# Statistics of the fourth row tile on ScalarE, those of the sixth and eighth on VectorE, and other ordering rules

## The chip, the cores and the metric

The kernel runs on one core of a Trainium2 chip. The engines are TensorE (PE, matmuls; PEld is its weight load), VectorE (DVE), ScalarE (ACT), GpSimd (POOL) and SyncE (SP, which issues DMAs). The metric is the device time of one execution in microseconds. Before the change it is 691.98 us, the median of three runs (691.73 to 692.18).

## The reference

One residual block on x of 2048 rows and 640 columns (bf16). The rows are normalised, and the result goes both through attention with 32 query heads of 20 columns and one shared key and value head, and through a two-layer network with silu:

```python
x = A_x
xn = _layernorm(x, axis=-1)
return x + _A_ref(xn, A_wq, A_wk, A_wv, A_wo) + _B_ref(xn, B_w1, B_w2)
```

In `_A_ref`, `q = xn @ wq` is split into 32 heads, `k = xn @ wk`, `v = xn @ wv`, `scores = q k^T * 20 ** -0.5`, and softmax over 2048 keys is taken before the product with v and with `wo`. In `_B_ref`, `h = silu(xn @ w1)` with 1728 columns, then `h @ w2`. The layernorm has no weights: `(x - m) / sqrt(v + 1e-5)`.

## The kernel before, in words

**Tiling.** The 2048 rows are 16 row tiles of 128, numbered from 0, and four query chunks of 512. Heads go in eight groups of four, each head in a slot of 32 rows, so that four score matmuls (`s_mm`, L1078) run side by side in TensorE. A unit of work is one key tile with one head: 128 keys by 512 queries, which fills one of the eight PSUM banks.

**The exponentials** are made on two ways. On ScalarE one ACTIVATE (L1166) takes two or three neighbouring banks, so 1024 or 1536 columns. On the other way a batch of four heads is turned by VectorE into integers that are read as bf16 (L1409, one head each), and two shifted copies of it are added, by GpSimd (L1448) or VectorE (L1453); the three together approximate the exponential, so such a batch needs three products with v where a batch of ScalarE needs one. The product with v is L1201 (`pv_mms`).

**Other matmuls.** Projections and the two layers go through `col_mm` (L447); `row_mm` (L454) is another cut of the same products that runs beside score matmuls. In the beginning each row tile is normalised, transposed (L595), copied into `xnT` by ScalarE for tiles 0 and 1 (L604) and by VectorE for the rest (L607); from that come kT (L621, copied by ScalarE at L631, and for tiles 1 to 3 by VectorE at L629), the first queries (L668, copied at L672), v (L645, L653) and the other queries (L447, L693). At the end stand the sums of the last head groups (copy L1302, matmuls L999, L1017) and the output layer (L919, L967, L984). Where TensorE would idle and has streamed little, a filler (L1725) multiplies zeros.

**The layernorm** (`ln_pair`) works on two row tiles at a time. A tile's statistics are made on VectorE (two BN_STATS, L563 and L565, one BN_AGGR, L567), or, for tiles in `ACT_LN`, on ScalarE: two ACTIVATEs with a sum over the row (L552, L554), after which VectorE scales the mean (L557). Then VectorE adds epsilon (L570), GpSimd takes the power -0.5 (L572), for tiles from 4 on VectorE forms a bias (L577), and the tile is normalised: tiles 0 to 3 by VectorE (L588), the others by GpSimd (L585). A pair goes on only when both of its tiles have their statistics. The ring of normalised tiles holds five.

**The order** of all instructions on every engine is made when the kernel is built. A list scheduler steps through modelled time, with a cost for each operation and a priority (`prio`), and picks the next operation of the engine that is earliest. TensorE's choice follows numbers in `BASE` (how long to keep a bank, how far products may lag, when to open a new sum). Every 10 us of modelled time (`PIECE`) the numbers are set anew: `BASE` with the exceptions in `RULES` that the letter of `PLAN` at that place names. Each engine then runs its list in order, with semaphore waits where another engine's result is needed. So a change to `PLAN`, or to the work of the beginning, makes another order for the whole kernel: which units go to ScalarE and which to VectorE, in which widths, and what stands between them on TensorE.

```python
while not finished():
    if sc.t["pe"] >= piece * PIECE:
        ru.__dict__.update(BASE)
        ru.__dict__.update(RULES[rule(piece)])
        piece += 1
```

The functions that the diff touches, with the line numbers of the profile:

Of the kernel before, what the change touches and what calls it, by code (L numbers as in the profile page):

```python
# [69 lines left out]
LOOK = 30.0  # L70
LOOK0 = 100.0
LOOK1 = 200.0
LNP = {1: ((4, 2), (6, 2)), 2: ((8, 2), (10, 2)), 3: ((12, 2), (14, 2))}
DVE_NORM = ()
PS = 1.0
# [23 lines left out]
AHEAD = 1  # L99
QAT = (0, 1)  # L100
TRN = 2
ACT_LN = (5, 7)
TRACT = (0, 1)

BASE = dict(uopen=4, umin=3, uleft=3, uwait=500.0, pace=-1.0, lagl=3, half=6, hold2=0, bnd=4, pj=6000.0, rows=0, rowmin=3, lagmax=6, lagp=0, lagj=6, openlag=5, late=-0.02, lead=0.01, leadmax=0.02, need=640.0, hold=300.0, dwant=600.0, slack=700.0, dnow=400.0, hungry=0.0, patience=0.0, keep=460.0, open=2, zcap=9, stay=0.0, homes=1, want=1, claim=6)
RULES = dict(a={}, b=dict(keep=0.0), c=dict(lagp=3), d=dict(lagp=5), e=dict(lagp=0), f=dict(patience=200.0), g=dict(dwant=0.0),
             h=dict(zcap=4), i=dict(zcap=3), j=dict(homes=0), k=dict(leadmax=-1.0, lead=-1.0), l=dict(lead=0.08, leadmax=0.1),
             m=dict(need=740.0), n=dict(hold=0.0), o=dict(stay=640.0), p=dict(open=1), q=dict(slack=560.0), r=dict(hungry=1000.0), s=dict(claim=9), t=dict(open=3), u=dict(claim=4), v=dict(want=2), w=dict(slack=850.0), x=dict(hold2=4), y=dict(bnd=0), z=dict(pj=-1e9), A=dict(rows=0), B=dict(rows=2, rowmin=2), C=dict(pj=2000.0), D=dict(openlag=3), E=dict(pj=8000.0), F=dict(hold2=3), G=dict(rows=1), H=dict(half=0), I=dict(half=3), J=dict(stay=560.0), K=dict(stay=720.0), P=dict(need=560.0), Q=dict(hold=120.0), L=dict(uopen=3), M=dict(uopen=4), N=dict(uopen=5), O=dict(uopen=0))
PLAN = "acbtJKazNvhaJvxvixrrnrKzDDnQDmoqvknpfLBGvDPmoJdftFQdkttaQBBoknQEaoz"


def rule(n):
    return PLAN[n] if n < len(PLAN) else "a"
PACE = 1.0
# [214 lines left out]
def build(nc, A_x, A_wq, A_wk, A_wv, A_wo, B_x, B_w1, B_w2, out, stack):  # L329
# [185 lines left out]
    def wrow(ap):  # L515
        return ap.rearrange("(c p) d -> p c d", p=P)
# [30 lines left out]
    def ln_pair(n0, k):  # L547
        aggs = []
        an = [n for n in range(n0, n0 + k) if n in ACT_LN]
        for n in an:  # L550
# [40 lines left out]
    def tr_job(n):  # L591
        mms = []
        for c in range(DC):
            def f(pe, b, c=c, n=n):
                return pe.transpose(bk16(b)[:, c * P:(c + 1) * P], xn_ring[n % XNR][:, c * P:(c + 1) * P],  # L595
                                    ident_b[:, :])
            mms.append((f, 65.0, "f", [norm_op[n], idb], [res("xn", n % XNR), res("idb")]))
        job = pe_job(f"tr{n}", mms, 550)

        def src(b):  # L600
            return bk16(b)[:, 0:DC * P].rearrange("p (c t) -> p c t", c=DC)
        dst = xnT[:, :, n * P:(n + 1) * P]
        if n in TRACT:
            op = Op("act", lambda a: a.activation(dst, src(job.bank), AF.Copy), t_act(640), ACT_END, pre=[job.ready],  # L604
                    writes=[res("xnT", n)], prio=-1.0, job=job)
        else:
            op = Op("dve", lambda v: v.tensor_copy(dst, src(job.bank)), 412, DVE_END, pre=[job.ready],  # L607
                    writes=[res("xnT", n)], prio=0.2 if n < 4 else PT, job=job)
        job.consumers = [op]
        xnT_op[n] = op  # L610
        return job
# [3 lines left out]
    def kT_job(t0, t1):  # L615
        mms = []
        parts = [(i, i + 1) for i in range(t0, t1)] if t1 <= 4 else [(t0, t1)]
        for a, b_ in parts:
            for c in range(DC):
                def f(pe, b, c=c, a=a, b_=b_):  # L620
                    return pe.matmul(bk(b, (a - t0) * P, (b_ - t0) * P), wk_sb[:, c, :], xnT[:, c, a * P:b_ * P],  # L621
                                     start=(c == 0), stop=(c == DC - 1))
                mms.append((f, t_mm((b_ - a) * P), "f", [xnT_op[i] for i in range(a, b_)] + wk_cp, [res("wk")]))
        job = pe_job(f"kT{t0}", mms, 1100)
        n = (t1 - t0) * P
        dst = kT_rep[:, t0 * P:t1 * P]
        args = dict(pre=[job.ready], writes=[res("kT", i) for i in range(t0, t1)], job=job)
        if t0 == 1:
            op = Op("dve", lambda v: v.tensor_copy(dst, bk(job.bank, 0, n)), t_dve(n), DVE_END, prio=0.25, **args)  # L629
        else:  # L630
            op = Op("act", lambda a: a.activation(dst, bk(job.bank, 0, n), AF.Copy), t_act(n), ACT_END, prio=-1.5, **args)  # L631
        job.consumers = [op]
        for i in range(t0, t1):
            kT_op[i] = op
        return job
# [27 lines left out]
    def q0_job(t0):  # L663
        mms = []
        for i in range(t0, t0 + 2):
            for c in range(DC):
                def f(pe, b, c=c, i=i):
                    return pe.matmul(bk(b, (i - t0) * P, (i - t0 + 1) * P), wq_pad[:, c, :], xnT[:, c, i * P:(i + 1) * P],  # L668
                                     start=(c == 0), stop=(c == DC - 1))
                mms.append((f, t_mm(P), "f", [xnT_op[i], wqp0], []))  # L670
        job = pe_job(f"q0_0{t0}", mms, 1100)
        op = Op("dve", lambda v: v.tensor_scalar_mul(qT[:, 0, t0 * P:(t0 + 2) * P], bk(job.bank, 0, 2 * P), QSCALE), t_dve(256), DVE_END,  # L672
                pre=[job.ready], writes=[res("qT", 0, 0, t0)], prio=0.2, job=job)
        job.consumers = [op]
        q_op.setdefault(0, []).append(op)
        q_res.setdefault(0, []).append(res("qT", 0, 0, t0))
        return job
# [797 lines left out]
    def pro_fill():  # L1475
        for kc in range(4):
            if kc == 0:
                ln_pair(0, 2)
                ln_pair(2, 2)
            else:  # L1480
                for a, k in LNP[kc]:
                    ln_pair(a, k)
            trs = []
            for n in range(4 * kc, 4 * kc + 4):
                j = tr_job(n)
                tr_ops[n] = j.ops
                trs.append(j)
            if kc == 0:
                ka, kb, qa, qb = kT_job(0, 1), kT_job(1, 4), q0_job(0), q0_job(2)
                ka.fixed, qa.fixed = ABUFS[1]  # L1490
                trs[2].fixed, trs[3].fixed, qb.fixed = ABUFS[0]
                pro.extend(Piece(j) for j in trs[:TRN])
                pro.append(Piece(ka))
                pro.append(Piece(qa, qa.ops[:DC]))
                pro.extend(Piece(j) for j in trs[TRN:])
                pro.append(Piece(qa, qa.ops[DC:]))
                pro.append(Piece(qb, qb.ops[:DC]))
                pro.append(Piece(qb, qb.ops[DC:]))
                pro.append(Piece(kb))
            else:  # L1500
                pro.extend(Piece(j) for j in trs)
                pro.append(Piece(kT_job(4 * kc, 4 * kc + 4)))
            pro.append(Piece(v_job(kc)))
            for k in range(2):
                if kc == QAT[k]:
                    pro.append(Piece(q_job(0, k)))
            if kc == 0:
                d_w["w1"] = dma("w1", lambda e: e.dma_start(w1_sb[:, :, :], wrow(B_w1)), D * F * 2, writes=[res("w1")],
                                prio=1.0)
                nf = (FC - 1) * P  # L1510
                d_w["w2a"] = dma("w2a", lambda e: e.dma_start(
                    w2_sb[:, 0:FC - 1, :], B_w2[0:nf, :].rearrange("(c p) d -> p c d", p=P)), nf * D * 2,
                    writes=[res("w2a")], prio=1.1)
                d_w["w2"] = dma("w2", lambda e: e.dma_start(w2_sb[0:FLAST, FC - 1, :], B_w2[nf:F, :]), FLAST * D * 2,
                                writes=[res("w2")], prio=1.2, pre=[d_w["w2a"]])
                d_w["w2b"] = dma("w2", lambda e: e.dma_start(w2_sb[FLAST:P, FC - 1, :], B_w2[nf:F, :]), FLAST * D * 2,
                                 writes=[res("w2b")], prio=1.2, pre=[d_w["w2"]])
                d_w["wo"] = dma("wo", lambda e: e.dma_start(wo_sb[:, :, :], wrow(A_wo)), D * D * 2, writes=[res("wo")],
                                prio=1.3)
                for k in range(2 * HG):  # L1520
                    a, r = (H - 2 * HG + k) * DH, k % HG * SLOT
                    d_wo_end.append(dma("wo_end", lambda e, k=k, a=a, r=r: e.dma_start(wo_end[r:r + DH, k // HG, :], A_wo[a:a + DH, :]),
                                        DH * D * 2, pre=[wo_zero], writes=[res("wo_end", k)], prio=1.4))
        for o in [d_w[k] for k in WLATE] + d_wo_end:
            o.pre += q_op[1]
        for i in range(QTP):
            xres_op[(0, i)] = x_ld[i]
# [436 lines left out]
    def step_other(e):  # L1964
        t = sc.t[e]
        best = None
        for op in sc.pools[e]:
            es = sc.est(op)
            if es is None:
                continue  # L1970
            key = (0, op.prio, es) if es <= t + ((LOOK0 if not att["n"] else LOOK if ln_done[0] else LOOK1) if op.prio < LOOKP else 30.0) else (1, es, op.prio)
            if best is None or key < best[0]:
# [201 lines left out]
```

## Time and profile before

| | |
|---|---|
| median of three runs | 691.98 us (691.73 to 692.18) |
| the profiled execution | 691.7 us, its span 689.9 us |
| busy share of the span | PE 98%, ACT 97%, DVE 86%, POOL 85% |
| exponentials on ScalarE | 590 of 1024 columns, 64 of 1536 |
| granted TensorE clock | 1.00 |

The span goes from the first instruction to the last; the profiled execution's own time has 1.8 us around it. A row of a timeline is start, duration (both us), engine, source line, operation, output and input with their shapes, the number of equal instructions merged, and in brackets the idle time before with what ended it. A row of a group ends with the busy time in us, the mean of one in ns, and the idle time before these instructions. A row of waits is total us, how often, and the longest. A row of stretches gives the length, then the busy us of PE, PEld, DVE, ACT and POOL with the number of instructions, the clock, the DMA share and GB/s. Neighbouring instructions of one engine can overlap by the tail of the first, so sums are taken from start to start.

### The profile page before, as it was taken

Reading aid. Unit: us, or ns where it says so; the run is one execution under the profiler, and the core shown is the slowest. Engines: PE = TensorE matmul, PEld = TensorE weight load, DVE = VectorE, ACT = ScalarE, POOL = GpSimd, SP = SyncE. Lnnn points to the kernel's source line nnn. Section 1 sums busy time; section 2 is a strip of 40 time slices with the busy share of each in tenths; the row PEclk is TensorE's granted clock in tenths of the full one; section 3 lists DMA queues with packets and bytes.
Section 4 is the critical chain, followed back from the end, with each engine's and each line's share of the span. In section 5 each row is a group of like instructions: output and inputs, shape, how many; then the busy total and the mean of one; then the engine's idle time right before and its main releaser. Section 6 shows DMA issues by size and latency. Waiting matters only on the chain.

```text
span 689.9 us, 22614 instructions
## 1 busy us (share of the span) xinstructions
PE 676.4 (98%) x9870; PEld 234.4 (34%) x9873; DVE 594.7 (86%) x1017; ACT 665.9 (97%) x726; POOL 583.9 (85%) x351
## 2 busy tenths in 40 slices
PE   8999999999999999999999999999999999999998
PEld 5432222322233333323233333322232333333345
DVE  7899989988998867898988888798988889989973
ACT  6999999999999999999999999999999999999990
POOL 6668899898988889898899899989889998888860
PEclk9999999999999999999999999999999999999999
DMA  7753221122221232321212223222222202223201
GB/s 217 178 180 42 20 20 15 33 35 30 18 28 12 31 40 30 69 34 17 33 14 30 29 31 40 23 65 29 29 19 22 22 18 32 31 23 68 23 7 41
DMA packets 34241, 28.97 MB, mean 42 GB/s; under 512 B 15486, under 2 KB 29662, under 8 KB 34142
## 3 DMA queue, kind: packets, MB, share of 16 engines
q1 hardware_dynamic: 33854, 27.20, 25.7%
q8 instruction: 77, 1.26, 0.8%
q10 hardware_dynamic: 288, 0.33, 0.1%
q14 instruction: 22, 0.18, 0.1%
HBM read 11.09 MB, written 2.62 MB: 20 GB/s over the span
## 4 chain that ended last, share of the span: by engine, by line
PE 76%; ACT 16%; DVE 4%; POOL 1%; SPq 1%; DMA 1%; issue 1%; DVEq 0%; ACTq 0%
PE psall L1201 26%; PE psall L1078 25%; PE psall L447 23%; ACT sbt L1166 14%; DVE sbt L1409 1%; ACT sbt L773 1%; POOL sbt L1448 1%; SPq L706 1%; DMA sbt<-sbt 0%; PE psall L621 0%; DVE sbt L563 0%; PE psall L734 0%; DVE sbt L607 0%; PE psall L1725 0%; DVE sbt L565 0%
## 5 line engine op out<-in xcount | busy, mean ns | idle before, releaser
L1166 ACT ACTIVATE sbt<-psall 128x1024 bf16<-128x1024 f32 (+1 forms) x654 | 643.0, 1156 | 2.3 <-PE psall L1078 2.1
L1448 POOL TENSOR_SCALAR sbt<-sbt 128x2048 int16<-128x2048 int16 x275 | 521.7, 1897 | 70.4 <-DVE sbt L1453 22.4
L1409 DVE TENSOR_SCALAR sbt<-psall 128x512 int16<-128x512 f32 x676 | 441.8, 685 | 64.4 <-PE psall L1078 60.1
L1078 PE MATMUL psall<-sbt 32*128 32x512 bf16 x2048 | 269.2, 384 | 4.3 <-ACT sbt L1166 1.6
L1201 PE MATMUL psall<-sbt 128*32 128x512 bf16 x3400 | 264.8, 384 | 0.6 <-POOL sbt L1448 0.4
L447 PE MATMUL psall<-sbt 128*32 128x320 bf16 (+3 forms) x3792 | 227.6, 332 | 2.5 <-DVE sbt L1409 0.8
L1078 PEld LDWEIGHTS psall<-sbt 32*128 32x128 bf16 x2048 | 71.4, 91 | 238.8 <-ACT sbt L1166 172.7
L447 PEld LDWEIGHTS psall<-sbt 128*32 128x32 bf16 (+1 forms) x3792 | 82.4, 95 | 82.7 <-issue 44.7
L1201 PEld LDWEIGHTS psall<-sbt 128*32 128x32 bf16 x3400 | 70.1, 94 | 114.5 <-issue 71.0
L1453 DVE TENSOR_SCALAR sbt<-sbt 128x2048 int16<-128x2048 int16 x63 | 48.6, 784 | 0.7 <-PE psall L1201 0.6
L860 POOL TENSOR_TENSOR sbt<-sbt 128x512 bf16<-128x512 f32 x30 | 38.2, 1274 | 7.2 <-DVE sbt L1453 5.5
L776 DVE SCALAR_TENSOR_TENSOR sbt<-sbt,psall 128x512 bf16<-128x512 bf16 x52 | 35.6, 684 | 5.2 <-ACT sbt L773 2.6
L773 ACT ACTIVATE sbt<-psall 128x512 bf16<-128x512 f32 x52 | 37.6, 723 | 0.1
L1250 DVE COPY sbt<-psall 128x512 f32<-128x512 f32 x31 | 21.2, 683 | 1.1 <-PE psall L1201 1.0
L454 PE MATMUL psall<-sbt 32*128 32x320 bf16 x70 | 21.3, 305 | 0.0
L1725 PE MATMUL psall<-sbt 128*32 128x256 bf16 (+1 forms) x228 | 14.4, 355 | 1.2 <-DVE sbt L487 1.2
L693 DVE TENSOR_SCALAR sbt<-psall 128x512 bf16<-128x512 f32 x20 | 13.6, 680 | 0.4 <-PE psall L447 0.4
L903 DVE SCALAR_TENSOR_TENSOR sbt<-psall,sbt 128x320 bf16<-128x320 f32 x24 | 11.6, 485 | 2.1 <-PE psall L447 1.6
L572 POOL TENSOR_TENSOR sbt<-sbt 128x2 f32<-128x2 f32 x8 | 5.7, 709 | 8.7 <-DVE sbt L570 8.3
L585 POOL TENSOR_SCALAR sbt<-sbt 128x640 bf16<-128x640 bf16 x12 | 10.4, 874 | 1.5 <-DVE sbt L577 1.5
L919 DVE SCALAR_TENSOR_TENSOR sbt<-psall,sbt 128x320 f32<-128x320 f32 x8 | 3.9, 486 | 8.0 <-PE psall L447 8.0
L1725 PEld LDWEIGHTS psall<-sbt 128*32 128x32 bf16 x228 | 7.0, 114 | 4.5 <-issue 1.6
(64 smaller groups left out, 117.9 us busy)
## 6 DMA issues: line engine op xcount, KB each, us to landing
sbt<-sbt SPq DMA_DIRECT2D x120, 64.0 KB, 3.9
sbt<-in_A_x_dram SPq DMA_DIRECT2D x28, 160.0 KB, 4.0
sbt<-sbt SPq DMA_DIRECT2D x213, 20.0 KB
out_dram<-sbt SPq DMA_DIRECT2D x14, 160.0 KB, 2.0
sbt<-in_B_w_dram SPq DMA_DIRECT2D x1, 2160.0 KB, 13.4
sbt<-in_B_w_dram SPq DMA_DIRECT2D x1, 2080.0 KB, 8.1
sbt<-sbt SPq DMA_DIRECT2D x75, 8.0 KB
sbt<-in_A_wq_dram SPq DMA_DIRECT2D x1, 800.0 KB, 5.9
```

The costliest lines, as they stand in the source:

```text
L447: ins = pe.matmul(ps[j * SLOT:(j + 1) * SLOT, b * BANK + off:b * BANK + off + n], w[:, j * SLOT:(j + 1) * SLOT], x, start=start, stop=stop ...
L454: return pe.matmul(ps[0:w.shape[-1], b * BANK:b * BANK + n], w[k], x[k], start=start, stop=stop, tile_position=(r * SLOT, 0))
L773: t = Op("act", lambda a: a.activation(t_buf[0:rows, ts, :], bk(job.bank, 0, QW, rows=rows), AF.Tanh, scale=0.5), t_act(512), ACT_END, pre ...
L776: u = Op("dve", lambda v: v.scalar_tensor_tensor(out=hT[par][0:rows, fk, :], in0=t_buf[0:rows, ts, :], scalar=1.0, in1=bk(job.bank, 0, QW, ...
L860: nm = pool(lambda e: e.tensor_tensor(oU[:, us, :], U_sb[:, us, :], Rrep, ALU.mult), 1356.0, POOL_END, pre=[uc] + lc + pack_op.get(divmod( ...
L1078: return pe.matmul(bk(b), kT_rep[i * SLOT:(i + 1) * SLOT, kt * P:(kt + 1) * P], qT[i * SLOT:(i + 1) * SLOT, g % NQ, :], start=True, stop=T ...
L1166: return a.activation(Ebuf[:, es * QW:es * QW + w], ps[:, buf[0] * BANK:buf[0] * BANK + w], AF.Exp, scale=ESCALE)
L1201: ins = pe.matmul(ps[i * SLOT:(i + 1) * SLOT, ub * BANK:ub * BANK + QW], lhsT, rhs, start=(first and k < HG), stop=(last and k >= len(lst) ...
L1409: p1 = Op("dve", lambda v: v.tensor_scalar(z16[:, i * QW:(i + 1) * QW], bk(job.bank), ZBIAS, 0.0, ALU.add, ALU.max), t_dve(QW) + 2.0, DVE_ ...
L1448: op = pool(lambda v, t=t, j=j, zin=zin: v.tensor_scalar(t.bitcast(I16), zin, float(SHIFT[j]), 1.0, ALU.add, ALU.mult), POOL_SHIFT, POOL_E ...
L1453: op = dve(lambda v, t=t, j=j, zin=zin: v.tensor_scalar_add(t.bitcast(I16), zin, float(SHIFT[j])), t_dve(N, 4), prio=SPRIO - 0.01 * j, **args)
L1725: ins = pe.matmul(ps[i * SLOT:(i + 1) * SLOT, ub * BANK:ub * BANK + n], zero_t[:, 0:SLOT], zero_t[:, 0:n], start=fresh, stop=fresh, tile_p ...
```

## The change

`ACT_LN` names tile 3 instead of tiles 5 and 7. The statistics of the fourth tile so move from VectorE to ScalarE, those of the sixth and eighth from ScalarE to VectorE. The first two calls of `ln_pair` take their pairs from a new constant, `LN0`, with the same pairs as before. `PLAN` is another string of as many letters.

```diff
+LN0 = ((0, 2), (2, 2))
...
-ACT_LN = (5, 7)
+ACT_LN = (3,)
...
-PLAN = "acbtJKazNvhaJvxvixrrnrKzDDnQDmoqvknpfLBGvDPmoJdftFQdkttaQBBoknQEaoz"
+PLAN = "aBbtOrBcFdxyoyvyQOowtQJJQwtoGJatntaEQtnqBozBzyayoriBHdtHaJnnqpJPJfgo"
...
             if kc == 0:
-                ln_pair(0, 2)
-                ln_pair(2, 2)
+                for a, k in LN0:
+                    ln_pair(a, k)
             else:
                 for a, k in LNP[kc]:
                     ln_pair(a, k)
```

Line numbers of the changed kernel are one higher from line 73 on.

## The prediction

> **What bounds the kernel now.** The first part of the page gives two engines nearly the whole span; the busy time by stretch, taken next, says which of them sets the pace, and where.
>
> ```profile
> PE 676.4 (98%) x9870; PEld 234.4 (34%) x9873; DVE 594.7 (86%) x1017; ACT 665.9 (97%) x726; POOL 583.9 (85%) x351
> 37.00:674.00 637.00, 630.90 (x9054) 206.30 (x9052) 558.54 (x910) 635.84 (x687) 562.05 (x310) 1.00 0.24 32
> 674.00:689.90 15.90, 12.60 (x344) 9.53 (x336) 6.13 (x12) 0.66 (x2) 0.20 (x1) 1.00 0.13 43
> ```
>
> From 37 us to 674 us ScalarE has 635.84 us of work in 637.00 us (the busy columns are PE, PEld, DVE, ACT, POOL). It is the bound there; TensorE is close but not full. After 674 us ScalarE is done and TensorE (12.60 of 15.90 us) sets the end. The waits of ScalarE and its largest groups, by shape, come third.
>
> ```profile
> ACT sbt L604 <- PE psall L595: 5.0, 1, 5.0
> ACT sbt L1166 <- PE psall L1078: 2.1, 6, 0.6
> L1166 ACT ACTIVATE sbt<-psall 128x1024 bf16<-128x1024 f32 x590 | 563.9, 1118 | 2.3 <-PE psall L1078 2.1
> L1166 ACT ACTIVATE sbt<-psall 128x1536 bf16<-128x1536 f32 x64 | 95.1, 1509 | 0.0
> ```
>
> All 654 exponentials together waited 2.1 us, in six places. So the span is: start of the first exponential, plus ScalarE's work from there, plus its few gaps, plus TensorE's rest after the last exponential. The timeline of ScalarE gives these.
>
> ```profile
> 10.03 0.73 ACT L552 ACTIVATE sbt<-sbt 128x640 bf16<-128x640 bf16 x1
> 10.88 0.83 ACT L554 ACTIVATE sbt<-sbt 128x640 bf16<-128x640 bf16 x1
> 13.59 1.92 ACT L1166 ACTIVATE sbt<-psall 128x1024 bf16<-128x1024 f32 x2
> 16.06 5.61 ACT L1166 ACTIVATE sbt<-psall 128x1024 bf16<-128x1024 f32 x6 [0.55 <-PE psall L1078]
> 21.50 0.66 ACT L631 ACTIVATE sbt<-psall 128x512 bf16<-128x512 f32 x1
> 22.64 7.44 ACT L1166 ACTIVATE sbt<-psall 128x1024 bf16<-128x1024 f32 x8 [0.48 <-PE psall L1078]
> 29.88 0.69 ACT L631 ACTIVATE sbt<-psall 128x512 bf16<-128x512 f32 x1
> 37.28 14.79 ACT L1166 ACTIVATE sbt<-psall 128x1024 bf16<-128x1024 f32 x16
> 51.78 0.79 ACT L773 ACTIVATE sbt<-psall 128x512 bf16<-128x512 f32 x1
> 663.15 10.44 ACT L1166 ACTIVATE sbt<-psall 128x1024 bf16<-128x1024 f32 x8
> 674.70 0.66 ACT L1302 ACTIVATE sbt<-psall 128x256 f32<-128x256 f32 x2 [1.11 <-PE psall L1201]
> ```
>
> The statistics of two tiles fill 10.03 to 13.59 us, 1.78 us a tile. Eight exponentials (two heads of keys 0 to 511 each) follow, then the copy of kT for row tiles 4 to 7 at 21.50, which the next exponentials need. Sixteen exponentials of 1024 columns take 51.78 - 37.28 = 14.50 us, 0.906 each. The last eight are one of 1024 and seven of 1536 in the order of instructions: (10.44 - 0.29 - 0.906) / 7 = 1.32 us each, 0.29 being what the sixteen show beyond their last start-to-start.
>
> **The change, part by part.** The order of instructions of the changed kernel, set against the one before, differs nearly everywhere, since the planner makes the whole order anew under other rules. What it adds up to: on ScalarE 579 exponentials of 1024 columns for 590, 74 of 1536 for 64, one tile's statistics for two; on VectorE one tile more of statistics, 8 fewer shifts out of the banks (L1409) and 3 fewer of L1453; one POOL shift fewer; on TensorE 16 matmuls of L1201 fewer and 52 of the filler (L1725) more. Two batches of four heads have gone from VectorE and GpSimd to ScalarE.
>
> *ScalarE's sum.* 10 x 1.32 - 11 x 0.906 = +3.2 us. Nothing hides it where ScalarE is the bound. With the group means' difference for 512 columns (1509 - 1118 = 391 ns) it would be +3.0, with time in proportion to the columns (1.36 each) +3.6: these are the ends. VectorE and GpSimd shed work they had idle time for, so nothing comes back there.
>
> *The fourth tile's statistics on ScalarE* lie in the 5.0 us that it waits for the first transposes: cost nothing, unless they run past the first copies at about 7.4 us; they take 1.78 us and can start when tile 3 lands, which had happened by 6.36 us at the latest (first row group below).
>
> *The beginning on VectorE.* These rows are of VectorE (at 6.36 tile 3's first half), the 13.03 one of TensorE:
>
> ```profile
> 6.23 0.21 DVE L567 BATCH_NORM_AGGREGATE sbt<-sbt 128x2 f32<-128x12 f32 x1
> 6.36 0.44 DVE L563 BATCH_NORM_STATS2 sbt<-sbt 128x6 f32<-128x320 bf16 x1
> 7.47 0.17 DVE L570 TENSOR_SCALAR sbt<-sbt 128x2 f32<-128x2 f32 x1
> 7.54 0.80 DVE L588 TENSOR_SCALAR sbt<-sbt 128x640 bf16<-128x640 bf16 x2
> 8.57 0.80 DVE L588 TENSOR_SCALAR sbt<-sbt 128x640 bf16<-128x640 bf16 x2 [0.23 <-POOL sbt L572]
> 9.41 0.49 DVE L563 BATCH_NORM_STATS2 sbt<-sbt 128x6 f32<-128x320 bf16 x1
> 9.82 0.48 DVE L565 BATCH_NORM_STATS2 sbt<-sbt 128x6 f32<-128x320 bf16 x1
> 10.99 0.42 DVE L672 TENSOR_SCALAR sbt<-psall 128x256 bf16<-128x256 f32 x1
> 13.03 0.40 PE L1078 MATMUL psall<-sbt 32*128 32x512 bf16 x4
> 14.07 0.55 DVE L629 CAST sbt<-psall 128x384 bf16<-128x384 f32 x1
> 17.85 0.87 DVE L607 COPY sbt<-psall 128x640 bf16<-128x640 bf16 x2
> ```
>
> Tile 3 leaves VectorE, so tiles 0 and 1 are normalised at 6.23 + 0.21 = 6.44 instead of 7.54. The second pair gains nothing: its variance line (L570) now stands behind those 0.80 us, at about 7.4 against 7.47, so it is normalised at 8.57 as before. But TensorE is through with the first pair by then, and the copies of tiles 2 and 3 (L607) no longer stand behind three half statistics of tiles 4 and 6: they begin at 9.4 instead of 10.6. I put the first score matmuls 1.4 us earlier, 11.6 for 13.03, and the first exponential at 12.1 for 13.59. Eight of 0.906 end at 19.4.
>
> There the price falls due. Tiles 4 to 7 are now all VectorE's. Between 9.37 and the variance line of tiles 4 and 5 stand two copies (0.8), two of L672 (0.75), five half statistics (0.40 from start to start), two aggregates (0.26), L629 (0.47) and some 0.2 of result latency: 13.85, against 12.02 before. These rows show what follows on GpSimd:
>
> ```profile
> 12.02 0.17 DVE L570 TENSOR_SCALAR sbt<-sbt 128x2 f32<-128x2 f32 x1
> 12.27 0.69 POOL L572 TENSOR_TENSOR sbt<-sbt 128x2 f32<-128x2 f32 x1 [3.73 <-DVE sbt L570]
> 12.99 0.16 DVE L577 SCALAR_TENSOR_TENSOR sbt<-sbt 128x2 f32<-128x2 f32 x1
> 13.27 0.88 POOL L585 TENSOR_SCALAR sbt<-sbt 128x640 bf16<-128x640 bf16 x1 [0.30 <-DVE sbt L577]
> 14.93 2.59 POOL L585 TENSOR_SCALAR sbt<-sbt 128x640 bf16<-128x640 bf16 x3
> ```
>
> The power (L572) comes 0.25 later, the first normalisation 1.00 after that: 15.1. Two take 1.73. The power of tiles 6 and 7, which stood between the first two normalisations, now stands behind both, so its 1.00 lies open: 17.83, and two more end at 19.56, where they ended at 14.93 + 2.59 = 17.52. Transpose (0.4), copy (0.49), five kT matmuls without score matmuls between them in the new order (0.22 each, as four of L1201 side by side take below) and three handovers of some 0.15 add 2.5: the kT copy stands at 22.1 instead of 21.50. ScalarE, done at 19.4, waits 2.7 us, and all that follows starts 0.6 later than before. Ends: -0.3, if the latencies overlap better, and +1.5, if the q copy and the four tile copies queue up on VectorE. For tiles 8 to 11 the same count ends the normalisations at 27.2 (before 25.5); kT is due when eight more exponentials end, at 30.5, so over 1 us is spare. SP's and GpSimd's other early work keeps its order. The filler costs nothing: it stands where TensorE waits.
>
> *The array's rate in that wait.* Two groups of TensorE, of 1 to 4 us and of 4 to 6.5 us:
>
> ```profile
> L1725 PE MATMUL psall<-sbt 128*32 128x256 bf16 x56 | 3.2, 419 | 1.2 <-DVE sbt L487 1.2
> L1725 PE MATMUL psall<-sbt 128*32 128x256 bf16 x72 | 3.0, 336 | 0.0
> ```
>
> The same matmul is slower at first (419 ns) than later, though the granted clock is 1.00 throughout. Score matmuls take 0.40 at 13.03 and 0.39 at 671.04, so the waits before 13 us had not brought the slow rate back. I take no cost. [...]
>
> *The end.* TensorE after the last score matmul (671.04 to 671.37):
>
> ```profile
> 671.04 0.39 PE L1078 MATMUL psall<-sbt 32*128 32x512 bf16 x3
> 671.37 3.28 PE L1201 MATMUL psall<-sbt 128*32 128x512 bf16 x56
> 674.48 2.89 PE L447 MATMUL psall<-sbt 128*32 128x320 bf16 x80
> 679.18 7.42 PE L447 MATMUL psall<-sbt 128*32 128x320 bf16 x212
> ```
>
> In the new order 20 of L1201 stand there for 56, and of L447 32 + 80 + 144 for 80 + 212. From these rows 0.0555 us each for L1201 ((674.48 - 671.37) / 56) and 0.035 for L447. Before the last exponential's own product now stand 16 x 0.0555 + 32 x 0.035 = 2.0 us, less than the two exponentials of 1.32 that are still to end, so that product waits for ScalarE and comes about 0.7 us sooner after the last score matmul; behind it 68 x 0.035 = 2.4 are gone. Together -3.1; ends -2.2 (if the sums or the last GpSimd shift are late) and -3.3 (all 36 + 36 matmuls).
>
> *The middle.* New order, same engines. Before, the waits there are at most the 2.1 us less the 0.55 and 0.48 of the rows above: 1.1 us. I take the same again; ends -0.4, and +3 for an order that fits less well.
>
> **The sum** against the profiled execution (span 689.9, its own time 691.7, which is 0.3 under the median 691.98 and at the lower edge of the runs): +0.6 +3.2 -3.1 +0 = +0.7, so 690.6 of span and 692.4 us.
>
> **Rivals.** *Slower: the new order makes ScalarE wait in the middle.* TensorE works in order, and a product waiting for a GpSimd shift of 1.9 us holds up the score matmuls behind it. For it: 637 us in which every wait is new. Against it: over 600 exponentials before with hardly a wait, by the same planner. Two waits of a microsecond decide; with +2.5 it gives 694.9. *Slower: the beginning is later than counted* (+1.5 for +0.6): 693.3, with late tiles 8 to 11 as well 694. [...] *Faster: the early exponentials are kept.* If tiles 6 and 7 are normalised by 18 us, the kT copy comes at 20.3, 1.2 before instead of 0.6 after: 690.6, and with a quieter middle 690.2. It decides from a copy before 20.5; the count of VectorE speaks against it. *The change does nothing at the start*: the kT copy at 21.5 again gives 691.8, inside the forecast.
>
> **How the numbers follow.** Within 0.2% of the median (690.6 to 693.4, about what a measurement of this kernel can tell from no change): 0.45. Middle 0.24, later beginning 0.07, slow array 0.03: slower 0.34. Kept exponentials or a better middle: faster 0.21. The range 690.1 to 695.0 reaches to both sides' rivals; the likeliest case alone has 691 to 693.6.
>
> **What would show it.** Right: first exponential near 12.1, a wait of 2 to 3 us before the kT copy at about 22.1, eight more heads on ScalarE, and 13 us from the end of the last exponential to the end where there were 16.3. Wrong: kT copy before 21, waits of ScalarE over 2 us after 37 us, or a tail as long as before.

## The result, and the profile after

The changed kernel takes 693.7 us (median of nine runs, 693.6 to 694.14), the kernel before, run beside it, 691.81 us (691.46 to 692.51). The ratio is 1.0029, with a 95% interval of 1.0020 to 1.0037: slower by 0.29%, 1.9 us. The profiled execution has a span of 691.9 us for 689.9 before.

The first part of the page of the changed kernel:

```profile
PE 680.1 (98%) x9903; PEld 234.1 (34%) x9903; DVE 588.9 (85%) x1007; ACT 668.0 (97%) x721; POOL 582.0 (84%) x350
```

Its busy time by stretch (length, then PE, PEld, DVE, ACT and POOL, granted clock, DMA share, GB/s):

```profile
37.00:674.00 637.00, 632.29 (x9079) 206.68 (x9082) 552.73 (x900) 635.83 (x684) 559.93 (x309) 1.00 0.24 32
674.00:691.90 17.90, 14.55 (x374) 9.89 (x366) 6.13 (x12) 5.08 (x6) 0.30 (x1) 1.00 0.12 39
```

From 37 to 674 us ScalarE is busy exactly as long as before (635.83 us for 635.84), so the middle has got no emptier and no fuller. It is not done at 674 us, however: 5.08 us of its work lie behind, where 0.66 lay before. Its waits:

```profile
ACT sbt L1167 <- PE psall L1079: 4.6, 4, 2.8
ACT sbt L632 <- PE psall L622: 3.1, 1, 3.1
```

its exponentials by shape

```profile
L1167 ACT ACTIVATE sbt<-psall 128x1024 bf16<-128x1024 f32 x579 | 554.5, 1116 | 4.3 <-PE psall L1079 3.9
L1167 ACT ACTIVATE sbt<-psall 128x1536 bf16<-128x1536 f32 x74 | 110.3, 1535 | 0.8 <-PE psall L1079 0.7
```

and its timeline (start, duration, with the wait ahead in brackets), the early part, the one listed wait of the middle, and the end:

```profile
11.82 7.44 ACT L1167 ACTIVATE sbt<-psall 128x1024 bf16<-128x1024 f32 x8 [2.84 <-PE psall L1079]
22.37 0.60 ACT L632 ACTIVATE sbt<-psall 128x512 bf16<-128x512 f32 x1 [3.11 <-PE psall L622]
23.52 7.44 ACT L1167 ACTIVATE sbt<-psall 128x1024 bf16<-128x1024 f32 x8 [0.55 <-PE psall L1079]
...
238.22 54.46 ACT L1167 ACTIVATE sbt<-psall 128x1536 bf16<-128x1536 f32 x56 [0.70 <-PE psall L1079]
...
659.02 19.40 ACT L1167 ACTIVATE sbt<-psall 128x1536 bf16<-128x1536 f32 x15
678.96 0.66 ACT L1303 ACTIVATE sbt<-psall 128x256 f32<-128x256 f32 x2 [0.54 <-PE psall L1202]
```

The 2.0 us of span can be read off these rows. The ninth exponential starts at 23.52, before at 22.64: +0.88. The last one ends at 659.02 + 19.40 = 678.42, before at 663.15 + 10.44 = 673.59: +4.83. From the last exponential to the end there are 691.9 - 678.42 = 13.5 us, before 16.3: -2.83. Between the ninth exponential and the last the listed waits are 1.19 us (the 0.70 above among them) for 1.03 (+0.16), which leaves 4.83 - 0.88 - 0.16 = 3.79 us of work and of lags too short to be listed. So +0.88 +3.79 +0.16 -2.83 = +2.0.

The tail on TensorE:

```profile
676.24 0.39 PE L1079 MATMUL psall<-sbt 32*128 32x512 bf16 x3
676.56 1.05 PE L1202 MATMUL psall<-sbt 128*32 128x512 bf16 x16
677.43 1.26 PE L448 MATMUL psall<-sbt 128*32 128x320 bf16 x32
678.52 0.39 PE L1202 MATMUL psall<-sbt 128*32 128x512 bf16 x4
678.74 2.89 PE L448 MATMUL psall<-sbt 128*32 128x320 bf16 x80
...
683.44 5.11 PE L448 MATMUL psall<-sbt 128*32 128x128 bf16 x144
```

The last product with an exponential (the four of L1202 at 678.52) stands right behind the last exponential, and the end has 144 matmuls of L448 in 5.11 us where there were 212 in 7.42.

### The profile page after: what moved, and what is told of

It is laid out like the page before. It is cut to its first block, busy times and chain, and to the rows that moved or that the text cites. A ratio compares the mean times of both kernels' runs of the same rounds, so it can differ in the third digit from the quotient of the medians.

```text
span 691.9 us, 22655 instructions
## 1 busy us (share of the span) xinstructions
PE 680.1 (98%) x9903; PEld 234.1 (34%) x9903; DVE 588.9 (85%) x1007; ACT 668.0 (97%) x721; POOL 582.0 (84%) x350
## 4 chain that ended last, share of the span: by engine, by line
ACT 66%; PE 29%; DVE 3%; DMA 0%; issue 0%; POOL 0%
ACT sbt L1167 62%; PE psall L448 9%; PE psall L1202 9%; PE psall L1079 9%; ACT sbt L774 4%; DVE sbt L1410 1%; DVE sbt L566 0%; DVE sbt L564 0%; PE psall L622 0%; DMA sbt<-in_A_x_dram 0%; DVE sbt L608 0%; PE psall L1018 0%; PE psall L596 0%; POOL sbt L573 0%; PE psall L669 0%
## 5 line engine op out<-in xcount | busy, mean ns | idle before, releaser
L1410 DVE TENSOR_SCALAR sbt<-psall 128x512 int16<-128x512 f32 x668 | 436.5, 684 | 70.6 <-PE psall L1079 66.2
L1202 PE MATMUL psall<-sbt 128*32 128x512 bf16 x3384 | 266.6, 384 | 2.1 <-ACT sbt L1167 0.5
L448 PE MATMUL psall<-sbt 128*32 128x320 bf16 (+3 forms) x3780 | 224.2, 332 | 1.4 <-DVE sbt L777 0.6
L448 PEld LDWEIGHTS psall<-sbt 128*32 128x32 bf16 (+1 forms) x3780 | 82.0, 95 | 83.6 <-issue 43.0
L1202 PEld LDWEIGHTS psall<-sbt 128*32 128x32 bf16 x3384 | 69.2, 94 | 115.7 <-issue 74.4
L1454 DVE TENSOR_SCALAR sbt<-sbt 128x2048 int16<-128x2048 int16 x60 | 46.3, 785 | 0.3 <-PE psall L1202 0.2
L455 PE MATMUL psall<-sbt 32*128 32x320 bf16 (+1 forms) x76 | 24.4, 321 | 0.0
L1726 PE MATMUL psall<-sbt 128*32 128x256 bf16 (+1 forms) x280 | 18.3, 349 | 1.2 <-DVE sbt L488 1.2
L694 DVE TENSOR_SCALAR sbt<-psall 128x512 bf16<-128x512 f32 x20 | 13.6, 678 | 0.4 <-PE psall L448 0.2
L904 DVE SCALAR_TENSOR_TENSOR sbt<-psall,sbt 128x320 bf16<-128x320 f32 x24 | 11.7, 486 | 2.3 <-PE psall L1079 1.4
```

Source lines behind the costliest of these rows:

```text
L448: ins = pe.matmul(ps[j * SLOT:(j + 1) * SLOT, b * BANK + off:b * BANK + off + n], w[:, j * SLOT:(j + 1) * SLOT], x, start=start, stop=stop ...
L455: return pe.matmul(ps[0:w.shape[-1], b * BANK:b * BANK + n], w[k], x[k], start=start, stop=stop, tile_position=(r * SLOT, 0))
L1202: ins = pe.matmul(ps[i * SLOT:(i + 1) * SLOT, ub * BANK:ub * BANK + QW], lhsT, rhs, start=(first and k < HG), stop=(last and k >= len(lst) ...
L1410: p1 = Op("dve", lambda v: v.tensor_scalar(z16[:, i * QW:(i + 1) * QW], bk(job.bank), ZBIAS, 0.0, ALU.add, ALU.max), t_dve(QW) + 2.0, DVE_ ...
L1454: op = dve(lambda v, t=t, j=j, zin=zin: v.tensor_scalar_add(t.bitcast(I16), zin, float(SHIFT[j])), t_dve(N, 4), prio=SPRIO - 0.01 * j, **args)
L1726: ins = pe.matmul(ps[i * SLOT:(i + 1) * SLOT, ub * BANK:ub * BANK + n], zero_t[:, 0:SLOT], zero_t[:, 0:n], start=fresh, stop=fresh, tile_p ...
```

## The experiments

Each kernel ran in five rounds beside the kernel before. The times below are medians, with the ratio to the kernel before and its 95% interval. The first four test terms of the sum: the start, the cause of its delay, and ScalarE's sum from both sides.

**Delay at the start alone.** The kernel before, with two more copies on ScalarE ahead of the copy of kT for row tiles 4 to 7.

```diff
+            def kcopy(a):
+                for lo, hi in ((0, 512), (512, 736)) if t0 == 4 else ():
+                    a.activation(scr[:, lo:hi], bk(job.bank, 0, hi - lo), AF.Copy)
+                return a.activation(dst, bk(job.bank, 0, n), AF.Copy)
-            op = Op("act", lambda a: a.activation(dst, bk(job.bank, 0, n), AF.Copy), t_act(n), ACT_END, prio=-1.5, **args)
+            op = Op("act", kcopy, t_act(n), ACT_END, prio=-1.5, **args)
```

> The kernel before, in the same order of instructions, with two more copies (512 and 224 columns, into a scratch tile that nothing reads) on ScalarE just ahead of the kT copy of tiles 4 to 7: 0.48 + 0.24 = 0.72 us from start to start. Theory (from the first kT copy on, ScalarE's stream sets the time, so a late start of it is paid one to one): +0.7 us against before, ratio about 1.001. Rival (TensorE and VectorE set the pace as much, and a late start of ScalarE is made up in the stream): within 0.2 us of before.

Measured: 692.36 us for 691.63, ratio 1.0010 (1.0001 to 1.0019): +0.73. In its trace the ninth exponential starts at 23.25 (before 22.64, +0.61), and from there to the last exponential the shift stays between 0.61 and 0.72 us. This delay at the start was paid in full; nothing later took it up.

**What holds the copy of kT.** The changed kernel with the statistics of row tiles 5 and 7 over 32 columns of each half.

```diff
-v.bn_stats(stats6[:, n, 0, :], xr(n)[:, 0:h2])
+v.bn_stats(stats6[:, n, 0, :], xr(n)[:, 0:32 if n in (5, 7) else h2])
...
-v.bn_stats(stats6[:, n, 1, :], xr(n)[:, h2:D])
+v.bn_stats(stats6[:, n, 1, :], xr(n)[:, h2:h2 + 32 if n in (5, 7) else D])
```

> The changed kernel, in the same order, with the statistics of tiles 5 and 7 taken over 32 columns of each half instead of 320, so that most of those two tiles' statistics is left out: four halves of about 0.12 instead of 0.40 us on VectorE, 1.1 us less. Theory (the wait of 3.1 us on ScalarE before the kT copy of tiles 4 to 7 comes from these statistics, by way of the power and the normalisations on GpSimd): the kT copy comes at 21.2 to 21.6 instead of 22.37, and the whole time falls by as much, 0.8 to 1.1 us against the changed kernel, about 692.7. Rival (that copy is held by the queue of q copy and tile copies on VectorE, or by TensorE): kT copy within 0.3 us of 22.37 and time within 0.3 us of the changed kernel's 693.7.

Measured: 693.67 us for 691.63, ratio 1.0036 (1.0024 to 1.0049), no gain on the changed kernel, as the rival had it. The beginning of the changed kernel, on GpSimd, VectorE and TensorE:

```profile
14.90 1.73 POOL L586 TENSOR_SCALAR sbt<-sbt 128x640 bf16<-128x640 bf16 x2 [0.31 <-DVE sbt L578]
17.48 0.39 PE L1079 MATMUL psall<-sbt 32*128 32x512 bf16 x2
17.73 1.73 POOL L586 TENSOR_SCALAR sbt<-sbt 128x640 bf16<-128x640 bf16 x2 [0.30 <-DVE sbt L578]
18.13 0.38 PE L455 MATMUL psall<-sbt 32*128 32x512 bf16 x1
18.45 0.73 PE L596 MATMUL psall<-sbt 128*128 128x128 bf16 x10
18.55 0.69 DVE L694 TENSOR_SCALAR sbt<-psall 128x512 bf16<-128x512 f32 x1
19.16 1.86 DVE L608 COPY sbt<-psall 128x640 bf16<-128x640 bf16 x4
21.08 1.25 PE L622 MATMUL psall<-sbt 128*128 128x512 bf16 x5 [0.26 <-DVE sbt L608]
```

and the same place in the experiment:

```profile
14.61 1.74 POOL L586 TENSOR_SCALAR sbt<-sbt 128x640 bf16<-128x640 bf16 x2 [0.31 <-DVE sbt L578]
17.45 1.74 POOL L586 TENSOR_SCALAR sbt<-sbt 128x640 bf16<-128x640 bf16 x2 [0.30 <-DVE sbt L578]
18.56 0.69 DVE L694 TENSOR_SCALAR sbt<-psall 128x512 bf16<-128x512 f32 x1 [0.34 <-PE psall L455]
19.16 1.86 DVE L608 COPY sbt<-psall 128x640 bf16<-128x640 bf16 x4
22.38 0.60 ACT L632 ACTIVATE sbt<-psall 128x512 bf16<-128x512 f32 x1 [3.11 <-PE psall L622]
```

The normalisations came 0.29 us sooner, the four tile copies on VectorE began at 19.16 and the copy of kT at 22.38 all the same. VectorE's L694 at 18.56 now shows what it waits for: TensorE's L455 at 18.13. That matmul and the score matmuls at 17.48 stand in TensorE's order ahead of the transposes (L596), and behind exponentials that ScalarE takes one by one. So the chain that was counted, statistics to power to normalisation, is not the one that ends last; the tiles' copies stand behind TensorE's row piece and VectorE's L694. Only 0.29 us of the 1.1 that were to come off reached the normalisations, so this shows which chain ends last, but not what a larger cut would do.

**ScalarE's sum, made longer.** The kernel before with eight more copies of 512 columns on ScalarE, spread over the middle (3.8 us).

```diff
             def ef(a):
+                if n >= 100 and n < 660 and n % 70 == 30:
+                    a.activation(scr[:, 0, :], bk(buf[0]), AF.Copy)
```

> The kernel before, in the same order, with eight more copies of 512 columns on ScalarE (into a scratch tile that nothing reads), each ahead of one exponential and some 60 us apart: 8 x 0.48 = 3.8 us. Theory (ScalarE is the bound of the middle and has no slack): +3.6 to +3.9 us, about 695.6. Rival (TensorE at 98% bounds it as much, ScalarE's work has slack): +1.5 or less.

Measured: 695.1 us for 691.63, ratio 1.0051 (1.0038 to 1.0064): +3.47 of 3.8. The work added to ScalarE in the middle was paid nearly in full.

**ScalarE's sum, made shorter.** The changed kernel with eight exponentials over 512 instead of 1024 columns.

```diff
             def ef(a):
+                if n >= 100 and n < 660 and n % 70 == 30 and len(buf) == 2:
+                    return a.activation(Ebuf[:, es * QW:es * QW + QW], bk(buf[0]), AF.Exp, scale=ESCALE)
```

> The changed kernel, in the same order, with eight of its exponentials, some 60 us apart, made over 512 columns instead of 1024, so that eight heads' exponentials are left out, the number by which the change raised ScalarE's share: 8 x 0.427 = 3.4 us less. Theory (ScalarE's eight more heads cost what they take): 3.2 to 3.4 us less than the changed kernel, about 690.4, below the kernel before. Rival (TensorE takes over as the bound as soon as ScalarE has less to do): at most 1.5 us less, above 692.

Measured: 693.26 us for 691.63, ratio 1.0024 (1.0014 to 1.0034): 0.44 us below the changed kernel, within the intervals of both, and the rival's number (above 692). By their starts in the trace, what followed a shortened exponential came 0.60 to 1.06 us after it, 0.82 on average, where 0.48 would have been possible and 0.90 to 1.06 was there without the cut. So the sum could be made longer at nearly the full price in the kernel before, but not shorter at the same price in the changed kernel; both ways in one kernel were not run. The next runs ask what holds it.

**TensorE made shorter, alone and together with ScalarE.** In the first of two kernels 20 shifted products with v are cut from 512 to 32 columns; the second has that and the eight shorter exponentials.

```diff
-                lst = [(v_all[:, j, kt, :], t[i], i) for i in range(HG)]
-                return pv_mms(pe, flags["bank"], lst, flags["first"], flags["last"])
+                n = 32 if j and nth % 17 == 8 and not flags["first"] else QW
+                lst = [(v_all[:, j, kt, :], t[i][..., 0:n], i) for i in range(HG)]
+                return pv_mms(pe, flags["bank"], lst, flags["first"], flags["last"], n)
```

> The changed kernel with 20 of the shifted products with v (80 matmuls) shortened from 512 columns to 32, spread over ten batches in the middle: about 20 x 0.20 = 4.1 us less work on TensorE (sixteen such matmuls took 0.87 us in the tail). Left out are 480 of the 512 columns of these products, so these heads' outputs lack a part. Theory (ScalarE's and TensorE's lists are both full): ScalarE's list is unchanged and still 3.8 us longer than before's, so little is won: 0 to -1 us, 692.7 to 693.7 us. Rival (TensorE's list alone holds the end since the shortening of eight exponentials won only 0.44 us): -3 to -4 us, 689.7 to 690.7 us.

> The changed kernel with both cuts: the 20 shortened products with v (-4.1 us of TensorE's work) and the eight exponentials over 512 instead of 1024 columns (-3.4 us of ScalarE's). Left out are those columns of the products and the second heads of those exponentials. Theory (both lists full): the two together win what neither wins alone, about the shorter of the two, -2 to -3.4 us, 690.3 to 691.7 us. Rival (TensorE alone): the same as with its own cut alone, within 0.5 us. Rival (neither: the time sits in the order's waits between engines): less than -1 us in sum.

Measured: 693.46 us (ratio 1.0031, 1.0020 to 1.0042) with TensorE's cut alone, 692.72 us (1.0014, 1.0005 to 1.0023) with both; the kernel before beside them 691.72. TensorE's work alone is not the bound either: 4.1 us less of it win 0.2. Both together win 1.0, which is more than each alone but at most half of what the theory wanted; the last rival (less than 1 us, the time sits in the order's waits) just has the number, with 0.98. The cuts did not stand in the same places, which leaves that open.

**Thirteen shorter tanh.** A place where the next scores have more time: the tanh of the hidden layer, which stand between exponentials, over 32 instead of 512 columns.

```diff
-        t = Op("act", lambda a: a.activation(t_buf[0:rows, ts, :], bk(job.bank, 0, QW, rows=rows), AF.Tanh, scale=0.5),
+        tn = 32 if qc >= 1 and (qc * FC + fk) % 3 == 2 else QW
+        t = Op("act", lambda a: a.activation(t_buf[0:rows, ts, 0:tn], bk(job.bank, 0, tn, rows=rows), AF.Tanh, scale=0.5),
```

> The changed kernel with 13 of the 52 tanh activations of the hidden layer (L774) over 32 instead of 512 columns: 13 x (0.477 - 0.18) = about 3.9 us less on ScalarE, at places between two exponentials, where the scores of the next exponential have had a whole exponential's time to be ready (0.82 us is what a shortened exponential's successor needed in the earlier run). Left out are 480 of the 512 columns of these tanh. Theory (ScalarE's list sets the pace, and the earlier cut of eight exponentials won little only because the next scores were not ready): -3 to -4 us, 689.7 to 690.7 us. Rival (TensorE's list is as long as ScalarE's, whatever is cut): within 1 us, 692.7 to 693.7 us.

Measured: 692.93 us for 691.97, ratio 1.0017 (1.0008 to 1.0026), 0.8 us below the changed kernel: the rival's number, although by the starts in the trace each short tanh took 0.08 us for 0.48 (0.18 was expected), 5.2 us in sum. One such place, ScalarE and TensorE in the changed kernel:

```profile
132.76 1.06 PE L1202 MATMUL psall<-sbt 128*32 128x512 bf16 x16
132.81 0.62 ACT L774 ACTIVATE sbt<-psall 128x512 bf16<-128x512 f32 x1
133.28 2.89 ACT L1167 ACTIVATE sbt<-psall 128x1024 bf16<-128x1024 f32 x3
133.75 0.39 PE L1079 MATMUL psall<-sbt 32*128 32x512 bf16 x3
```

and with the shorter tanh:

```profile
132.72 1.11 PE L1203 MATMUL psall<-sbt 128*32 128x512 bf16 x16
132.82 0.22 ACT L775 ACTIVATE sbt<-psall 128x32 bf16<-128x32 f32 x1
132.90 1.05 ACT L1168 ACTIVATE sbt<-psall 128x1024 bf16<-128x1024 f32 x1
133.76 0.39 PE L1080 MATMUL psall<-sbt 32*128 32x512 bf16 x3
134.19 3.77 ACT L1168 ACTIVATE sbt<-psall 128x1024 bf16<-128x1024 f32 x4 [0.24 <-PE psall L1080]
```

The exponential behind the tanh starts 0.38 us sooner (132.90 for 133.28). The score matmuls for the one after it stay where they were (133.76 for 133.75), because sixteen products stand ahead of them in TensorE's order, in the time that the tanh had left. So that exponential starts at 134.19, and the gain is gone one instruction later. At this place TensorE's order is as tight as ScalarE's. Set beside the changed kernel's trace, all thirteen places go this way: the instruction behind each short tanh starts 0.39 to 0.40 us sooner, and at the third instruction behind it 0.00 to 0.30 us of that is left, 0.09 on average.

**Much room on TensorE.** 1336 matmuls of the shifted products over 256 instead of 512 columns, all through the program; and the same with the thirteen shorter tanh.

```diff
+                n = 256 if j and not flags["first"] else QW
+                lst = [(v_all[:, j, kt, :], t[i][..., 0:n], i) for i in range(HG)]
```

> The changed kernel with 1336 of the shifted products' matmuls over 256 instead of 512 columns, all through the program: 1336 x 0.027 = about 36 us less work on TensorE (sixteen of 512 columns took 0.87 us in the tail), with every other list and ScalarE's order as in the changed kernel. Left out is half of each of these products. In the changed kernel's trace the exponentials of 1024 columns follow each other at 0.904 us at the median and at 0.976 us at the ninth decile; summed over the middle the starts lag by about 10 us behind 0.906 and 1.33 us per exponential. Theory (both lists are full, TensorE's order makes these lags): most of the 10 us goes, 684 to 688 us. Rival (the lags come from the turn of the score banks between ScalarE and TensorE or from VectorE and GpSimd, not from TensorE's amount of work): within 2 us, 691.7 to 694 us.

> The kernel of the last run (1336 shifted products halved, 36 us less on TensorE, 691.9 us) with the 13 tanh activations over 32 instead of 512 columns as well: 13 x (0.478 - 0.078) = 5.2 us less on ScalarE by the starts measured in the run that cut these tanh alone, where they won 0.8 us. Left out are half of those products and 480 columns of those tanh. Theory (ScalarE's and TensorE's lists are both full, so that a cut shows once TensorE has room): most of the 5.2 us shows, -3.5 to -5.2 us against 691.9, that is 686.7 to 688.4 us, below the kernel before. Rival (a third thing paces the middle: the turn of the score banks, VectorE or GpSimd): -0.8 us or less won again, 691.1 to 691.9 us.

Measured: 691.89 us for 691.82 (1.0002, 0.9993 to 1.0011), and with the tanh 691.17 for 691.87 (0.9992, 0.9983 to 1.0001). Some 36 us less on TensorE win 1.8 us, and the tanh won no more with them (0.7) than without (0.8). The room on TensorE is real, though its busy time hides most of it. From 37 to 674 us, with TensorE alone:

```profile
37.00:674.00 637.00, 619.70 (x9095) 1.00 0.24 32
```

That is 12.6 us less than the changed kernel's 632.29, while by their starts four of the halved products took 0.12 us for 0.23, 36 us in sum. The theory that two full lists of work hold each other falls: the amount of TensorE's work is not what holds the middle. What the rows at 132 to 134 us above do show is a matter of order: the scores for the next exponential stand behind products that TensorE may not overtake. At 132.76 those sixteen products were of the kind that this experiment left whole, so it hardly loosened that place: with both cuts, 0.14 us of the 0.40 is left at the third instruction behind a short tanh, on the average of the thirteen. Whether the rest is the same thing elsewhere, or the turn of the score banks (TensorE's score matmuls waited for ScalarE's exponentials 4.3 us in this run, in 20 places; 0.82 us on average is what followed a shortened exponential), stays open.

**Without the fillers.** The changed kernel without the 144 filler matmuls that stand behind the beginning.

```diff
-                    prog[e].append(("n", op.fn, None))
+                    prog[e].append(("n", op.fn, "fill" if op.name == "fill" and op.seq > 200 else None))
...
+            elif kind == "n" and b == "fill":
+                pass
```

> The changed kernel without the filler matmuls after the beginning (100 of 512 columns and 44 of 256, about 6.6 us of TensorE's work by 0.054 us for 512 columns). The output is whole. If the fillers stand only where TensorE would wait anyway, 693.7 us +-0.4. If some of them delay the S products that ScalarE waits for, down to the 2.9 us by which the changed kernel's fillers exceed the old one's: 690.8 to 693 us.

Measured: 696.41 us for 691.72, ratio 1.0064 (1.0051 to 1.0077): 2.7 us slower than with them. Neither case had that. A short stretch of the changed kernel, and then three of this one, with TensorE alone (length, PE busy, granted clock, DMA share, GB/s):

```profile
214.00:218.00 4.00, 3.59 (x44) 1.00 0.09 21
...
214.00:218.00 4.00, 2.64 (x25) 0.94 0.06 15
218.00:222.00 4.00, 4.00 (x32) 0.50 0.04 7
222.00:226.00 4.00, 4.00 (x58) 0.70 0.04 6
```

and score matmuls in the last three, on the timeline:

```profile
216.09 0.39 PE L1079 MATMUL psall<-sbt 32*128 32x512 bf16 x3 [0.53 <-ACT sbt L1167]
218.45 0.61 PE L1079 MATMUL psall<-sbt 32*128 32x512 bf16 x2
```

The granted clock falls to 0.50 for about 7 us (an estimate from the 0.94, 0.50 and 0.70 of the three stretches), the score matmuls take 0.61 us for 0.39, and by the starts of the score matmuls 2.7 us are lost there; the same happens near 30 us (clock 0.50 over 30 to 32 us, 0.69 over 32 to 34), with 1.3 us lost. The changed kernel has a clock of 1.00 in both places, so in these executions the clock fell there without the fillers and stayed with them. Not every execution of this kernel fell twice: the five took 695.0, 695.0, 696.4, 696.7 and 697.6 us with a mean granted clock of 0.998, 0.998, 0.995, 0.995 and 0.992, which is about what one fall of 1.3 us, one of 2.7, and both would give; the profiled one is the last. Away from the two places its exponentials keep their distance to the changed kernel's within 0.04 us, so the fillers themselves cost nothing there.

**Each half of the change alone.** The new beginning with the old string of rules, and the old beginning with the new string.

```diff
-ACT_LN = (3,)
+ACT_LN = (5, 7)
```

That is the edit of the second, made in the changed kernel; the first is the changed kernel with the old PLAN.

> The new beginning (fourth row tile on ScalarE) with the old string of rules. Its order has 566 exponentials of 1024 columns and 89 of 1536 on ScalarE (before 590 and 64): 566 x 0.906 + 89 x 1.33 + 0.5 = 631.7 us against 619.7, +12.0 us; 28 heads fewer on VectorE. Theory (ScalarE's sum sets the end of its list, the tail gives back 3 to 10 us): 694.7 to 702 us. Rival (the beginning alone is the cost, the string only fine tuning): 692.4 to 693.0 us.

> The old beginning (sixth and eighth row tile on ScalarE) with the new string of rules. Its order has 556 exponentials of 1024 columns and 96 of 1536: 556 x 0.906 + 96 x 1.33 = 631.4 us against 619.7, +11.7 us; 28 heads fewer on VectorE. Theory (ScalarE's sum, the tail gives back 3 to 10 us): 693.5 to 700.5 us. Rival (the beginning alone is the cost): 691.8 +-0.5 us.

Measured: 706.42 us (ratio 1.0209, 1.0195 to 1.0223) and 709.6 us (1.0252, 1.0238 to 1.0266), the kernel before beside them 691.97. The waits of ScalarE's exponentials after 37 us, for the new beginning with the old string,

```profile
ACT sbt L1167 <- PE psall L1079: 5.0, 7, 1.9
```

its last exponentials on the timeline,

```profile
638.70 51.78 ACT L1167 ACTIVATE sbt<-psall 128x1536 bf16<-128x1536 f32 x52 [1.90 <-PE psall L1079]
```

and, for the old beginning with the new string, the same waits and then the last exponentials:

```profile
ACT sbt L1167 <- PE psall L1079: 10.4, 12, 2.8
```

```profile
681.43 15.07 ACT L1167 ACTIVATE sbt<-psall 128x1024 bf16<-128x1024 f32 x14 [0.63 <-PE psall L1079]
```

With the same accounts as above, the first has its last exponential end at 690.48, 16.9 us later than before: +0.5 from the start, +12.0 by its count of exponentials, +4.6 of waits (5.0 for 0.4) make 17.1. Its tail is 13.9 us, 2.4 shorter; together +14.5, as measured. The second: 696.50, 22.9 later; +11.7 by the count and +10.0 of waits leave 1.3 unaccounted for; its tail is 11.0 us, 5.3 shorter; together +17.6. So the account of span that the prediction used holds in orders that are far apart. In the second kernel the granted clock was 0.99 from 150 to 300 us and from 300 to 450 us, 1.00 in the changed kernel; how much of its waits and of the 1.3 us comes from that is not separated. The theory had left out the waits in the middle, and the "fine tuning" rival is off by 14 and 18 us: a string of rules belongs to the beginning that it was made for.

## Why the prediction was right, and where it was wrong

693.7 us lies in the range of 690.1 to 695.0, but just outside the likeliest case's own 691 to 693.6 and outside "within 0.2%" (up to 693.4). The sign that had 0.34 came true, not the one that had 0.45. The range is 4.9 us wide for a change of 1.9, so whether the mechanism was right is told by the terms and not by the hit. Term by term, with the predicted number first:

- **The start, +0.6; measured +0.88.** The first exponential came at 11.82 (12.1), eight of them ended at 19.26 (19.4), ScalarE waited 3.1 us (2.7) and copied kT at 22.37 (22.1). The normalisations stood where they were counted (14.90 for 15.1, the last end at 19.46 for 19.56). The cause named for the delay, the statistics, power and normalisation of tiles 4 to 7, failed: normalising 0.29 us sooner moved nothing. What the prediction had put at the upper end of this term, that "the q copy and the four tile copies queue up on VectorE", is what the rows show, behind a matmul of TensorE. That the 0.6 was nearly right is in part luck: two chains happened to be of about the same length.
- **ScalarE's sum, +3.2 (3.0 to 3.6); measured 3.79.** This is the largest of the four misses. The prices were right: by starts in the trace 0.904 us for 1024 columns and 1.330 for 1536 are the medians, and 10 x 1.330 - 11 x 0.906 is +3.33. The other 0.46 us are lags too short to be listed as waits, which the prediction had not priced. That ScalarE's longer work is paid nearly in full was right (3.47 of 3.8 when added on purpose).
- **The tail, -3.1; measured -2.83.** The last product comes right behind the last exponential, and the end is shorter by the 68 matmuls of L448, as counted. No run tested this term by itself.
- **The middle, 0; measured +0.16** of listed waits, 0.70 in one place. The slower rival (waits in the middle) did not come true here; in both kernels that had one half of the change it did, with 4.6 and 10.0 us.
- **"TensorE is close but not full"** is right as to the amount of work (36 us less of it win 1.8). What it did not say is that the order on TensorE is tight around ScalarE's, so that time taken off ScalarE is not given back: cuts of 3.4 and 5.2 us won 0.4 and 0.8. The profile page's chain of the work that ended last, whose links are inferred, fits that: it runs through TensorE for 76% of the span and ScalarE for 16% before, and through ScalarE for 66% and TensorE for 29% after, so it names neither engine alone as the pace of either kernel.
- **"The filler costs nothing"** holds away from the two falls of the clock, by the distances above. The reason given (it stands where TensorE waits) is half of it: without the later fillers the kernel is 2.7 us slower.
- **The slow array**, the term with the chance of 0.03, is shown by no run: in the waits at 20 us the granted clock is 1.00 (18 to 24 us), and the score matmuls on either side, at 17.48 and 23.09, take 0.39 us. What the runs showed in its place is a fall in mid-run, which the trace of before does not have: in the run without fillers the clock was 0.50 from 218 to 222 us, with score matmuls of 0.61 us for 0.39.

The sum was thus +0.7 for a measured +2.0: +0.28 from the start, +0.59 from ScalarE's sum, +0.16 from the middle and +0.27 from the tail. Each is small; all four had the same sign.

## What to carry to other kernels

When two terms of several microseconds cancel (here +4.8 at the last exponential and -2.8 in the tail), the sign of the rest is worth no more than the sum of the small errors, so lags below the threshold of the list of waits need a price too. A bound shown by adding work (paid in full) is not yet shown to give the time back when work is taken away: try both, and look at the next few instructions behind the cut to see who holds them. An order made by a planner belongs to its beginning; a change to the one is measured only with the other made anew.

## What the runs showed of the hardware that was not expected

In the run without fillers TensorE's granted clock fell to 0.50 although it never stood idle for long: from 214 to 218 us it was busy 2.64 of 4.00 us (3.59 in the changed kernel, with a clock of 1.00), and the longest of its waits there was 0.53 us. The clock of 0.50 lasted about 7 us and cost 2.7. What sets such a fall off these rows do not show. The run with the shorter statistics and the one with much room on TensorE each had the clock down near 518 us (0.50 and 0.61 over 518 to 520 us) in the profiled execution. The first lost 1.5 us there: its tanh at 515.62 stood 0.03 us behind the changed kernel's, the next, at 524.92 for 523.41, 1.51. The profiled execution of the second took 1.2 us more than the median (693.08 for 691.89). The first of them had TensorE busy 1.96 of 2.00 us from 514 to 516 us and 1.79 from 516 to 518, with a clock of 1.00 and then 0.75; the changed kernel, with the same order, was busy the same 1.96 and 1.79 us and kept 1.00. The old beginning with the new string had its 0.99 with its fillers in place. What decides at such a place stays open.
